# A convolution, SwiGLU and ELU kernel on one core: a lag of two units in the joined stage, DMA landings reckoned by size, and GpSimd as the maker of some convolution taps

## The chip, the cores and the metric

The kernel runs on one core of one Trainium2 chip. The metric is the device time of one launch in microseconds (us); smaller is better. An engine of the core (TensorE, VectorE, ScalarE, GpSimd; PE, DVE, ACT, POOL in the rows) works through a queue of its own in order, and an instruction that waits for a semaphore holds up all that stands behind it in that queue. SyncE (SP) issues the DMAs, also in order.

## What is computed

```python
x_unf = x_pad[:, idx, :].reshape(B, S, K, H, group)      # B=2, S=4096, D=192, K=7, H=8
out = np.einsum('hk,bskhg->bshg', softmax(weight), x_unf)  # a causal convolution of 7 taps, one set per head
x = out.reshape(B * S, D)                                  # 8192 tokens of 192 channels
x = (silu(x @ w_gate) * (x @ w_val)) @ w_out               # d_ff = 1536
h = x @ w_in                                               # d_ff = 2048
out = np.where(h > 0, h, np.exp(np.minimum(h, 0)) - 1) @ w_out2
```

The weights come as float64, the tokens as float32. Products are made to float32 precision from pieces: each operand is split in a high part (`hi`, type fp32r) and a rest (`lo`), and three of the four products are summed.

## The kernel before

**Blocks, units and pairs.** The tokens are cut into 16 blocks of 512. Channels lie on the partitions: 0:128 in a 128x512 tile, 128:192 in halves. A unit of layer 1, written (1, b, j) or s(b, j) here, is block b times 128 columns of d_ff: `swiglu(b, j)` makes two PSUM tiles, `pg` and `pv`, with nine couples of matmuls (`Into.nine`, L363), each couple two matmuls on the two 64-row halves of the array at once. A couple is called a pair below. ACT takes silu of `pg` (L679), DVE multiplies by `pv` (`gate`, L683), `split` makes hi on ACT (L653) and lo on DVE (L657), and `products_out` adds the unit's five pairs (`OutOf.ten`, L406) to the four sums `c` of the block. There are 12 units per block in layer 1, and 16 in layer 2 (`elus`, two at a time).

**Preparation.** A block's x comes by DMA (`load_x`, L519). `conv(b, 0)` makes channels 0:128: the first tap on ACT (L574), six more on DVE (L577, multiply and add in one instruction). `conv(b, 1)` makes channels 128:192 in the same way at 256 columns; for blocks 0 and 1 TensorE does that part with diagonal matrices (`products`, L553, tile `pc`). Then hi and lo are cut (L450 and L454 for 128x512, L475 and L478 for the halves), and DMAs from SBUF to SBUF copy halves across partitions (`turn`, L497; `send`, L491), so that each half of the array has its rows.

**Weights.** Each of the 34 pieces (`piece`) is brought once by DMA (L263; four moves of 64 partitions, or one of 384 KB), put together from the words of float64 by ACT (L267, L290) and DVE (L294, L275), and split into hi on ACT (L299) and lo on DVE (L302). All of it is done in the first 120 us, beside the matmuls of blocks 0 and 1.

**Order.** Nothing is scheduled by hand. `plan.add` records each operation with its engine, an estimated pitch (how long it holds its engine) and an estimated `ready` time (when its result is there); `Plan.run` walks through the estimates and emits instructions in the order that comes out, longest remaining path first among those that can start. TensorE's order alone is the order in which the units are written (`behind` links each PE task to the one before). An instruction that comes later than estimated still stands at its place in the queue.

**The joined stage.** `both_first` writes blocks 0 and 1 of layer 1 together, since the weights come too slowly for one block alone: units of block 0 alone up to j = JOINED, then one of block 1 after each one of block 0. `due` holds units whose `products_out` is not written yet:

```python
for j in range(NU[1]):
    swiglu(0, j)
    if due:
        for u in due.pop(0):
            products_out(u)
    due.append([(1, 0, j)])
    if j >= JOINED:
        swiglu(1, done)
```

So with the lag of one, TensorE's order is s(0,0), s(0,1), products of (0,0), s(0,2), products of (0,1), and so on.

Of the kernel before, what the change touches and what calls it, by code (L numbers as in the profile page):

```python
# [7 lines left out]
F32 = mybir.dt.float32  # L8
# [4 lines left out]
ALU = mybir.AluOpType  # L13
# [3 lines left out]
P = 128  # L17
# [3 lines left out]
LEAD = 3  # L21
AIDED = 1
PATIENCE = 0.05
JOINED = 4
EPS = 2.0**-16
SPARED = range(0, 34)

# [5 lines left out]
class Task:  # L33
# [3 lines left out]
    def __init__(self, engine, pitch, ready, emit):  # L37
        self.engine, self.pitch, self.ready, self.emit = engine, pitch, ready, emit
        self.drain = 0.05 if engine in ("act", "dve") else 0.0
        self.needs, self.behind, self.left, self.next, self.at, self.tail = [], [], 0, [], None, 0.0  # L40


class Plan:
# [60 lines left out]
    def run(self, free, patience):  # L104

        self.link()
        waiting = {e: [] for e in free}
        for t in self.tasks:
            if not t.left:
                waiting[t.engine].append((0.0, t))  # L110
        count = 0
        while any(waiting.values()):
            when, e = min((max(free[e], min(a for a, _ in w)), e) for e, w in waiting.items() if w)
            can = [(a, t) for a, t in waiting[e] if a <= when + patience]
            a, t = max(can, key=lambda c: c[1].tail)
            waiting[e].remove((a, t))
            t.at = max(when, a)
            free[e] = t.at + t.pitch
            t.emit()
            count += 1  # L120
            for d in t.next:
                d.left -= 1
                if not d.left:
                    at = 0.0
                    for q in d.needs:
                        at = max(at, q.at + (q.pitch + q.drain if q.engine == d.engine else q.ready))
                    for q in d.behind:
                        at = max(at, q.at)
                    waiting[d.engine].append((at, d))
        assert count == len(self.tasks)  # L130
# [3 lines left out]
def tile_conv_swiglu_elu(ctx: ExitStack, tc: tile.TileContext, x, weight, words, out, FF1, FF2):  # L134
# [42 lines left out]
    def pool(emit, needs=(), new=(), uses=(), pitch=1.45, ready=1.6):  # L177
        return plan.add("pool", pitch, ready, emit, needs, new, uses)

    def move(emit, needs=(), new=(), uses=(), pitch=0.62, ready=2.9):  # L180
        return plan.add("sp", pitch, ready, emit, needs, new, uses)

    def couple(emit, needs=(), new=(), uses=()):
        return plan.add("pe", 0.233, 0.64, emit, needs, new, uses)
# [65 lines left out]
    def piece(k, moves, halves, serves):  # L250
# [50 lines left out]
        def lo_part(pick, hi, lo):  # L301
            nc.vector.tensor_tensor(out=lo, in0=pick(box["f"]), in1=raw(hi), op=ALU.subtract)  # L302

        came = [
            move(lambda i=i: bring(i), new=[st_b] if i == 0 else (), uses=[] if i == 0 else [st_b], ready=3.3)
            for i in range(len(moves))
        ]
        for i in came[1:]:
# [111 lines left out]
    class Operand:  # L420
# [25 lines left out]
        def write(self, s, value, needs, uses, n):  # L446


            def hi():
                nc.scalar.copy(self.tile(0)[:, s, :n], value())  # L450

            def lo():
                v, h = value(), self.tiles[0][:, s, :n]
                nc.vector.tensor_tensor(out=self.tile(1)[:, s, :n], in0=v, in1=raw(h), op=ALU.subtract)  # L454

            h = self.task(0, act, hi, needs, uses)
            l = self.task(1, dve, lo, [*needs, h], [self.bufs[0], *uses])
            self.slots[0, s], self.slots[1, s] = [h], [l]
            if s == 0:
                for q, done in ((0, h), (1, l)):  # L460
                    self.slots[q, 1] = [
                        move(lambda q=q, r=r, r_in=r_in: turn(self.tiles[q], r, r_in, n), [done], uses=[self.bufs[q]])
                        for r, r_in in ((lower, upper), (upper, lower))
                    ]

        def spread(self, value, done, buf, n):


            half = n // 2
            places = (lower, slice(0, half)), (upper, slice(half, n))  # L470
            his, los = [], []
            for r, c in places:

                def hi(r=r, c=c):
                    nc.scalar.copy(self.tile(0)[r, 2, c], value()[r, :half])  # L475

                def lo(r=r, c=c):
                    nc.vector.tensor_tensor(  # L478
                        out=self.tile(1)[r, 2, c], in0=value()[r, :half], in1=raw(self.tiles[0][r, 2, c]), op=ALU.subtract
                    )  # L480

                h = self.task(0, act, hi, [done], [buf], pitch=0.33, ready=0.45)
                l = self.task(1, dve, lo, [done, h], [self.bufs[0], buf], pitch=0.34, ready=0.47)
                his.append(h)
                los.append(l)
            for q, own in enumerate((his, los)):
                other = []
                for (r, c), (r_in, _), t in zip(places, places[::-1], own):

                    def send(q=q, r=r, c=c, r_in=r_in):  # L490
                        nc.sync.dma_start(out=raw(self.tiles[q][r_in, 2, c]), in_=raw(self.tiles[q][r, 2, c]))  # L491

                    other.append(move(send, [t], uses=[self.bufs[q]]))
                self.slots[q, 2] = [*own, *other]

    def turn(t, r, r_in, n):
# [2 lines left out]
    def load_x(b):  # L499
# [12 lines left out]
        def bring(k):  # L512
# [6 lines left out]
            nc.sync.dma_start(out=at(k, skip, HALO + m), in_=src)  # L519

        came = [
            move(lambda k=k: bring(k), new=[] if k else [buf], uses=[buf] if k else [], ready=3.2) for k in range(3)
        ]
        pads = []
        if a:
# [11 lines left out]
    def products(b):  # L537
# [20 lines left out]
            t = plan.add("pe", cost, cost + 0.4, lambda k=k: product(k), [diagonals[k], *came[1]], **new)  # L558
        X[b].spread(lambda: box["p"], t, bank, n)

    def conv(b, g):

        n = blocks[b][2]
        m, c0 = ((n, 0), (n // 2, HALO + TB))[g]
        src, src_b, came = xs[b]
        acc_b = plan.buffer("cv", 2)
        box = {}

        def tap(k):
            s = src["t"][:, c0 + k : c0 + k + m]  # L570
            w = taps[:, g, k : k + 1]
            if k == HALO:
                box["acc"] = cv_p.tile([P, TB], F32, tag="cv", name=f"cv{b}_{g}")
                nc.scalar.mul(box["acc"][:, :m], s, w)  # L574
                return
            acc = box["acc"][:, :m]
            nc.vector.scalar_tensor_tensor(out=acc, in0=s, scalar=w, in1=acc, op0=ALU.mult, op1=ALU.add)  # L577

        less = 0.0 if g == 0 else 0.27
        t = act(lambda: tap(HALO), [made, *came[g]], new=[acc_b], uses=[src_b], pitch=0.62 - less, ready=0.78 - less)  # L580
        for k in range(HALO):
            t = dve(lambda k=k: tap(k), [t], uses=[src_b, acc_b], pitch=0.67 - less, ready=0.8 - less)
        if g == 0:
            if b not in X:
                X[b] = Operand(f"x{b}", home["x", b])
            X[b].write(0, lambda: box["acc"][:, :n], [t], [acc_b], n)
        else:
            X[b].spread(lambda: box["acc"], t, acc_b, n)
# [281 lines left out]
    def both_first():  # L870
# [3 lines left out]
        waiting = []  # L874
        for j in range(NU[1]):
            swiglu(0, j)
            if due:
                for u in due.pop(0):
                    products_out(u)
            due.append([(1, 0, j)])  # L880
            if j >= JOINED:
                swiglu(1, done)
                waiting.append([(1, 1, done)])
                done += 1
# [82 lines left out]
```

## Time and profile before

| | |
|---|---|
| median of 3 runs | 1224.97 us (1223.95 to 1226.94) |
| the profiled execution | 1224.98 us |
| its span, first to last instruction | 1223.2 us (so 1.8 us lie around it) |
| TensorE busy in the span | 1208.4 us (99%) |
| VectorE busy | 981.6 us (80%) |
| ScalarE busy | 833.7 us (68%) |
| GpSimd busy | 2.1 us |
| DMA from HBM, mean over the span | 21 GB/s read and written |

TensorE is busy nearly throughout, so time can be won or lost only where it waits: at the start, and at waits inside. VectorE's 80% is a mean over a start in which it is nearly full and a long rest in which it is not. The rows give the start of an instruction in us from the span's start, how long it took, the idle time of its engine just before it in brackets, and what ended that.

### The profile page before, as it was taken

The page shows a single profiled execution, that of the slowest core. Times are in us where ns is not written, and L with a number is a line of the kernel's source. Part 1 is how long each engine was busy: PE and PEld are TensorE (multiplying, and loading weights), DVE is VectorE, ACT ScalarE, POOL GpSimd, SP SyncE. Part 2 cuts the span into 40 slices and gives each one's busy share as a digit, 9 for nine tenths or more (in the row PEclk, how much of TensorE's full clock was granted, in tenths as well). Part 3 has the DMA queues.
Part 4 walks back from the last instruction along what each step waited for, and adds up shares of the span by engine and source line. Part 5 has one row for each costly group of instructions (what it writes and reads, how often), then busy time and mean ns, then how long its engine had stood idle before and what let it go on. Part 6 is the DMA issues. An engine that isn't in the chain of part 4 may idle for free.

```text
span 1223.2 us, 25355 instructions
## 1 busy us (share of the span) xinstructions
PE 1208.4 (99%) x10272; PEld 1023.3 (84%) x10272; DVE 981.6 (80%) x1631; ACT 833.7 (68%) x1556; POOL 2.1 (0%) x15
## 2 busy tenths in 40 slices
PE   7999999999999999999999999999999999999998
PEld 5878888999999999988888888878878888888876
DVE  8899899788595986959779596895968869495697
ACT  7878687486683856748576484765848667385676
POOL 0000000000000000000000000000000000000000
PEclk9999999999999999999999999999999999999999
DMA  5736020202020020201102011020200102000000
GB/s 162 200 95 162 15 44 14 66 18 53 1 44 27 18 53 8 50 15 25 47 10 49 14 36 36 18 53 1 44 14 18 40 1 48 11 18 14 18 10 18
DMA packets 34917, 48.65 MB, mean 40 GB/s; under 512 B 5872, under 2 KB 19696, under 8 KB 34800
## 3 DMA queue, kind: packets, MB, share of 16 engines
q1 hardware_dynamic: 34784, 47.04, 15.2%
q8 instruction: 80, 1.31, 0.5%
q14 instruction: 37, 0.30, 0.1%
q10 hardware_dynamic: 16, 0.00, 0.0%
HBM read 19.75 MB, written 6.29 MB: 21 GB/s over the span
## 4 chain that ended last, share of the span: by engine, by line
PE 88%; DVE 4%; ACT 3%; DMA 2%; SPq 1%; issue 1%; ACTq 0%; DVEq 0%
PE c L406 39%; PE pv L363 21%; PE ph L363 20%; PE pg L363 7%; DMA words<-in_words_dram 2%; DVE t L721 1%; SPq L263 1%; DVE t L725 1%; DVE h L657 1%; DVE cv L577 1%; ACT t L679 0%; DVE t L683 0%; ACT words L290 0%; ACT h L653 0%; SPq L519 0%
## 5 line engine op out<-in xcount | busy, mean ns | idle before, releaser
L406 PE MATMUL c<-h,out 64*128 64x512 f32 x4400 | 624.2, 392 | 2.7 <-ACT h L653 1.7
L406 PEld LDWEIGHTS c<-h,out 64*128 64x128 f32 x4400 | 482.4, 185 | 82.6 <-DVE o L762 3.7
L653 ACT CAST h<-t 128x512 fp32r<-128x512 f32 x440 | 274.2, 624 | 172.0 <-DVE t L683 124.3
L363 PE MATMUL pv<-x,in1hi 64*128 64x512 f32 x1152 | 390.6, 393 | 0.4 <-DVE t L683 0.3
L363 PE MATMUL pg<-x,in1hi 64*128 64x512 f32 x1152 | 390.0, 393 | 0.5 <-ACT in1hi L299 0.5
L657 DVE TENSOR_TENSOR h<-t,h 128x512 fp32r<-128x512 f32 x440 | 302.8, 688 | 92.4 <-ACT h L653 89.4
L363 PE MATMUL ph<-y,in2hi 64*128 64x512 f32 x1536 | 316.4, 391 | 0.0
L363 PEld LDWEIGHTS ph<-y,in2hi 64*128 64x128 f32 x1536 | 234.2, 185 | 26.9 <-DVE t L725 0.8
L363 PEld LDWEIGHTS pv<-x,in1hi 64*128 64x128 f32 x1152 | 213.2, 185 | 33.5 <-DVE t L683 1.3
L363 PE MATMUL ph<-y,in2lo 64*128 64x512 f32 x768 | 233.8, 391 | 0.0
L363 PE MATMUL pg<-x,in1lo 64*128 64x512 f32 x576 | 226.1, 393 | 0.8 <-DVE in1lo L302 0.8
L363 PE MATMUL pv<-x,in1lo 64*128 64x512 f32 x576 | 226.2, 393 | 0.0
L683 DVE TENSOR_TENSOR t<-t,pv 128x512 f32<-128x512 f32 x192 | 131.6, 685 | 117.7 <-ACT t L679 117.4
L363 PEld LDWEIGHTS pg<-x,in1hi 64*128 64x128 f32 x1152 | 213.1, 185 | 8.3 <-ACT in1hi L299 1.3
L679 ACT ACTIVATE t<-pg 128x512 f32<-128x512 f32 x192 | 114.6, 597 | 148.8 <-PE pg L363 142.2
L721 DVE SCALAR_TENSOR_TENSOR t<-t,th 128x512 f32<-128x512 f32 x256 | 175.7, 687 | 9.7 <-ACT t L717 9.2
L725 DVE SCALAR_TENSOR_TENSOR t<-ph,t 128x512 f32<-128x512 f32 x256 | 172.1, 688 | 3.0
L713 ACT ACTIVATE th<-ph 128x512 f32<-128x512 f32 x256 | 153.7, 600 | 24.5 <-PE ph L363 23.6
L717 ACT ACTIVATE t<-ph 128x512 f32<-128x512 f32 x256 | 153.9, 601 | 0.0
L363 PEld LDWEIGHTS ph<-y,in2lo 64*128 64x128 f32 x768 | 137.3, 185 | 12.4
L363 PEld LDWEIGHTS pv<-x,in1lo 64*128 64x128 f32 x576 | 106.7, 185 | 16.4
L363 PEld LDWEIGHTS pg<-x,in1lo 64*128 64x128 f32 x576 | 106.7, 185 | 5.1 <-DVE in1lo L302 1.6
(66 smaller groups left out, 566.1 us busy)
## 6 DMA issues: line engine op xcount, KB each, us to landing
x<-x SPq DMA_DIRECT2D x64, 128.0 KB, 3.4
y<-y SPq DMA_DIRECT2D x64, 128.0 KB, 2.3
words<-in_words_dram SPq DMA_DIRECT2D x14, 384.0 KB, 3.9
words<-in_words_dram SPq DMA_DIRECT2D x40, 128.0 KB, 3.0
x<-x SPq DMA_DIRECT2D x64, 64.0 KB, 2.0
out_dram<-o SPq DMA_DIRECT2D x16, 256.0 KB, 2.0
xs<-in_x_dram SPq DMA_DIRECT2D x14, 259.0 KB, 2.9
words<-in_words_dram SPq DMA_DIRECT2D x40, 64.0 KB, 2.6
```

The costliest lines, as they stand in the source:

```text
L263: nc.sync.dma_start(out=to[r, g], in_=w[r_in, g_in])
L363: nc.tensor.matmul(p[:, :n], w[r, k, s], m[r, s, :n], start=i == 0, stop=i == len(seq) - 1)
L406: nc.tensor.matmul(p[:, :n], lhs[r], m[r, :n], start=start, stop=stop)
L577: nc.vector.scalar_tensor_tensor(out=acc, in0=s, scalar=w, in1=acc, op0=ALU.mult, op1=ALU.add)
L653: nc.scalar.copy(parts[u][0][:, :n], live[u][0]["t"][:, :n])
L657: nc.vector.tensor_tensor(out=parts[u][1][:, :n], in0=live[u][0]["t"][:, :n], in1=raw(parts[u][0][:, :n]), op=ALU.subtract)
L679: nc.scalar.activation(out=box["t"][:, :n], in_=box["p"][0][:, :n], func=AF.Silu)
L683: nc.vector.tensor_tensor(out=t, in0=t, in1=box["p"][1][:, :n], op=ALU.mult)
L713: nc.scalar.activation(out=own["th"][:, :n], in_=box["p"][a][:, :n], func=AF.Tanh, scale=0.5)
L717: nc.scalar.activation(out=own["t"][:, :n], in_=box["p"][a][:, :n], func=AF.Exp)
L721: nc.vector.scalar_tensor_tensor(out=t, in0=t, scalar=1.0, in1=th, op0=ALU.add, op1=ALU.mult)
L725: nc.vector.scalar_tensor_tensor(out=t, in0=box["p"][a][:, :n], scalar=0.0, in1=t, op0=ALU.max, op1=ALU.min)
```

## The change

Four things are edited; all else is as before.

1. **The lag** in `both_first`: `if due:` becomes `if len(due) > 1:`, so a unit's products are written two units after it. JOINED goes from 4 to 5: one unit more of block 0 stands alone ahead of the first unit of block 1.
2. **Landings by size**: `move` takes `kb`, and `Plan.run` reckons a DMA's landing from a running total (`flow`) instead of a fixed time after its issue. These are estimates: they change the order that is emitted, not a transfer.
3. **`calm`**: in blocks 1 and 2 (`CALM`), `conv(b, 0)`, and in block 2 `conv(b, 1)` too, are made by GpSimd: one multiplication for the first tap, then six times a multiplication into a tile `by` and an addition to the sum. ACT's L574 and the six L577 of DVE fall away for each of these three (two of 128x512, one of 128x256). The later steps (hi on ACT, lo on DVE, the copies) stay.
4. The pitches of some moves are given apart (0.45 or 0.60 for 0.62).

```diff
--- before.py
+++ after.py
@@ -21,7 +21,9 @@
 LEAD = 3
 AIDED = 1
 PATIENCE = 0.05
-JOINED = 4
+CALM = (1, 2)
+FLOW = 250
+JOINED = 5
 EPS = 2.0**-16
 SPARED = range(0, 34)
 
@@ -37,6 +39,7 @@
     def __init__(self, engine, pitch, ready, emit):
         self.engine, self.pitch, self.ready, self.emit = engine, pitch, ready, emit
         self.drain = 0.05 if engine in ("act", "dve") else 0.0
+        self.kb = 0
         self.needs, self.behind, self.left, self.next, self.at, self.tail = [], [], 0, [], None, 0.0
 
 
@@ -108,7 +111,7 @@
         for t in self.tasks:
             if not t.left:
                 waiting[t.engine].append((0.0, t))
-        count = 0
+        count, flow = 0, 0.0
         while any(waiting.values()):
             when, e = min((max(free[e], min(a for a, _ in w)), e) for e, w in waiting.items() if w)
             can = [(a, t) for a, t in waiting[e] if a <= when + patience]
@@ -116,6 +119,9 @@
             waiting[e].remove((a, t))
             t.at = max(when, a)
             free[e] = t.at + t.pitch
+            if t.kb:
+                flow = max(t.at + t.pitch + 0.9, flow) + t.kb / FLOW
+                t.ready = flow + 0.4 - t.at
             t.emit()
             count += 1
             for d in t.next:
@@ -177,8 +183,10 @@
     def pool(emit, needs=(), new=(), uses=(), pitch=1.45, ready=1.6):
         return plan.add("pool", pitch, ready, emit, needs, new, uses)
 
-    def move(emit, needs=(), new=(), uses=(), pitch=0.62, ready=2.9):
-        return plan.add("sp", pitch, ready, emit, needs, new, uses)
+    def move(emit, needs=(), new=(), uses=(), pitch=0.62, ready=2.9, kb=0):
+        t = plan.add("sp", pitch, ready, emit, needs, new, uses)
+        t.kb = kb
+        return t
 
     def couple(emit, needs=(), new=(), uses=()):
         return plan.add("pe", 0.233, 0.64, emit, needs, new, uses)
@@ -302,7 +310,10 @@
             nc.vector.tensor_tensor(out=lo, in0=pick(box["f"]), in1=raw(hi), op=ALU.subtract)
 
         came = [
-            move(lambda i=i: bring(i), new=[st_b] if i == 0 else (), uses=[] if i == 0 else [st_b], ready=3.3)
+            move(
+                lambda i=i: bring(i), new=[st_b] if i == 0 else (), uses=[] if i == 0 else [st_b], ready=3.3,
+                kb=(160, 80, 160, 80)[i] if len(moves) > 1 else 384, pitch=0.62 if len(moves) > 1 else 0.45,
+            )
             for i in range(len(moves))
         ]
         for i in came[1:]:
@@ -459,7 +470,8 @@
             if s == 0:
                 for q, done in ((0, h), (1, l)):
                     self.slots[q, 1] = [
-                        move(lambda q=q, r=r, r_in=r_in: turn(self.tiles[q], r, r_in, n), [done], uses=[self.bufs[q]])
+                        move(lambda q=q, r=r, r_in=r_in: turn(self.tiles[q], r, r_in, n), [done], uses=[self.bufs[q]],
+                             kb=150)
                         for r, r_in in ((lower, upper), (upper, lower))
                     ]
 
@@ -490,7 +502,7 @@
                     def send(q=q, r=r, c=c, r_in=r_in):
                         nc.sync.dma_start(out=raw(self.tiles[q][r_in, 2, c]), in_=raw(self.tiles[q][r, 2, c]))
 
-                    other.append(move(send, [t], uses=[self.bufs[q]]))
+                    other.append(move(send, [t], uses=[self.bufs[q]], kb=75))
                 self.slots[q, 2] = [*own, *other]
 
     def turn(t, r, r_in, n):
@@ -519,7 +531,8 @@
             nc.sync.dma_start(out=at(k, skip, HALO + m), in_=src)
 
         came = [
-            move(lambda k=k: bring(k), new=[] if k else [buf], uses=[buf] if k else [], ready=3.2) for k in range(3)
+            move(lambda k=k: bring(k), new=[] if k else [buf], uses=[buf] if k else [], ready=3.2,
+                 kb=65 if k else 259, pitch=0.6 if k else 0.45) for k in range(3)
         ]
         pads = []
         if a:
@@ -558,6 +571,36 @@
             t = plan.add("pe", cost, cost + 0.4, lambda k=k: product(k), [diagonals[k], *came[1]], **new)
         X[b].spread(lambda: box["p"], t, bank, n)
 
+    def calm(box, src, src_b, acc_b, came, g, m, c0, b):
+
+
+
+        of = lambda k: (src["t"][:, c0 + k : c0 + k + m], taps[:, g, k : k + 1])
+        by_b = plan.buffer("th", 2)
+
+        def begin():
+            box["acc"] = cv_p.tile([P, TB], F32, tag="cv", name=f"cv{b}_{g}")
+            s, w = of(HALO)
+            nc.gpsimd.tensor_scalar_mul(out=box["acc"][:, :m], in0=s, scalar1=w)
+
+        def scaled(k):
+            if k == 0:
+                box["by"] = th_p.tile([P, TB], F32, tag="th", name=f"by{b}_{g}")
+            s, w = of(k)
+            nc.gpsimd.tensor_scalar_mul(out=box["by"][:, :m], in0=s, scalar1=w)
+
+        def added():
+            acc = box["acc"][:, :m]
+            nc.gpsimd.tensor_tensor(out=acc, in0=acc, in1=box["by"][:, :m], op=ALU.add)
+
+        one, two = 0.1 + 0.0014 * m, 0.1 + 0.0024 * m
+        t = pool(begin, [made, *came[g]], new=[acc_b], uses=[src_b], pitch=one, ready=one + 0.15)
+        for k in range(HALO):
+            place = dict(uses=[src_b, by_b]) if k else dict(uses=[src_b], new=[by_b])
+            t = pool(lambda k=k: scaled(k), [t], pitch=one, ready=one + 0.15, **place)
+            t = pool(added, [t], uses=[acc_b, by_b], pitch=two, ready=two + 0.15)
+        return t
+
     def conv(b, g):
 
         n = blocks[b][2]
@@ -577,9 +620,14 @@
             nc.vector.scalar_tensor_tensor(out=acc, in0=s, scalar=w, in1=acc, op0=ALU.mult, op1=ALU.add)
 
         less = 0.0 if g == 0 else 0.27
-        t = act(lambda: tap(HALO), [made, *came[g]], new=[acc_b], uses=[src_b], pitch=0.62 - less, ready=0.78 - less)
-        for k in range(HALO):
-            t = dve(lambda k=k: tap(k), [t], uses=[src_b, acc_b], pitch=0.67 - less, ready=0.8 - less)
+        if b in CALM:
+            t = calm(box, src, src_b, acc_b, came, g, m, c0, b)
+        else:
+            t = act(
+                lambda: tap(HALO), [made, *came[g]], new=[acc_b], uses=[src_b], pitch=0.62 - less, ready=0.78 - less
+            )
+            for k in range(HALO):
+                t = dve(lambda k=k: tap(k), [t], uses=[src_b, acc_b], pitch=0.67 - less, ready=0.8 - less)
         if g == 0:
             if b not in X:
                 X[b] = Operand(f"x{b}", home["x", b])
@@ -874,7 +922,7 @@
         waiting = []
         for j in range(NU[1]):
             swiglu(0, j)
-            if due:
+            if len(due) > 1:
                 for u in due.pop(0):
                     products_out(u)
             due.append([(1, 0, j)])
```

What this does to the order, read from the built programs of the two kernels. **On PE**, just behind unit s(0,1). The names are those of the program: `pg0_1` is the gate tile of block 0, unit 1; `x00` and `x01` are the hi and lo parts of block 0's x; `c1_0_k` are the sums of layer 1, block 0. Before:

```order
L363 MATMUL pg0_1_269<-x01_200,in1hi_114 128x512
L363 MATMUL pv0_1_270<-x01_200,in1hi_114 128x512
L406 MATMUL c1_0_0_308<-h0_1_0_0_298,out1_118 128x512
L406 MATMUL c1_0_1_309<-h0_1_0_0_298,out1_118 128x512
L406 MATMUL c1_0_0_308<-h1_1_0_0_306,out1_118 128x512
```

and now:

```order
L374 MATMUL pg0_1_282<-x01_206,in1hi_114 128x512
L374 MATMUL pv0_1_283<-x01_206,in1hi_114 128x512
L374 MATMUL pg0_2_315<-x00_198,in1hi_114 128x512
L374 MATMUL pv0_2_316<-x00_198,in1hi_114 128x512
L374 MATMUL pg0_2_315<-x00_198,in1lo_115 128x512
```

The nine pairs of s(0,2) stand ahead of the products of (0,0), which follow behind them.

**On ACT**, around the hi of block 0's x (`words0`, `w0` and so on are pieces of weights; `pc0` is the TensorE-made part of x). Before:

```order
L267 ACTIVATE w0_189<-words0_136 128x384
L450 CAST x00_193<-cv0_0_153 128x512
L290 ACTIVATE words0_136<-words0_136 128x384
L475 CAST x00_193<-pc0_157 64x256 x2
L290 ACTIVATE words1_173<-words1_173 128x384
L267 ACTIVATE w1_216<-words1_173 128x384
L299 CAST in1hi_114<-w0_189 128x384
```

and now:

```order
L275 ACTIVATE w0_187<-words0_134 128x384
L298 ACTIVATE words0_134<-words0_134 128x384
L461 CAST x00_198<-cv0_0_154 128x512
L298 ACTIVATE words1_169<-words1_169 128x384
L307 CAST in1hi_114<-w0_187 128x384
L487 CAST x00_198<-pc0_156 64x256 x2
```

The hi of the first piece of weights stands ahead of the `pc0` part of x now, and so does an instruction that waits for `words1` to land.

**On ACT**, where the hi of block 2's x stands (`cv2_0` and `cv2_1` are the sums that GpSimd makes now; `t1_0_11` and `h0_1_0_11` belong to the last unit of block 0). Before:

```order
L679 ACTIVATE t1_0_11_1071<-pg0_11_1040 128x512
L450 CAST x20_1080<-cv2_0_735 128x512
L653 CAST h0_1_0_11_1097<-t1_0_11_1071 128x512
L679 ACTIVATE t1_1_7_1118<-pg1_7_1082 128x512
L475 CAST x20_1080<-cv2_1_862 64x256 x2
```

and now:

```order
L727 ACTIVATE t1_0_11_1078<-pg0_11_1035 128x512
L461 CAST x20_1086<-cv2_0_740 128x512
L487 CAST x20_1086<-cv2_1_867 64x256
L701 CAST h0_1_0_11_1109<-t1_0_11_1078 128x512
L487 CAST x20_1086<-cv2_1_867 64x256
L617 ACTIVATE cv3_0_1123<-xs3_766,taps_106 128x512
L727 ACTIVATE t1_1_6_1135<-pg1_6_1089 128x512
```

The silu of unit s(1,6) and the hi of (0,11) stand behind two instructions that wait for GpSimd's sums.

## Rows read from the trace of the kernel before

**Rows 1.** The page's first part: busy us, share of the span, instructions.
```profile
PE 1208.4 (99%) x10272; PEld 1023.3 (84%) x10272; DVE 981.6 (80%) x1631; ACT 833.7 (68%) x1556; POOL 2.1 (0%) x15
```
**Rows 2.** Windows: us, busy by engine, granted clock (PEclk), DMA share, GB/s.
```profile
15.00:37.00 22.00, 18.68 (x130) 13.54 (x132) 19.86 (x38) 14.90 (x32) 0.00 (x0) 0.92 0.63 167
60.00:75.00 15.00, 14.67 (x123) 11.28 (x121) 14.90 (x28) 11.49 (x25) 0.00 (x0) 1.00 0.24 75
75.00:120.00 45.00, 44.37 (x380) 35.63 (x378) 43.93 (x88) 38.20 (x82) 0.00 (x0) 1.00 0.59 155
```
**Rows 3.** The timeline of PE, 5 to 30 us: start, us, instruction, idle before.
```profile
5.77 9.10 PE L553 MATMUL pc<-xs,tapped 128*128 128x256 f32 x28 [0.91 <-ACT tapped L544]
...
15.42 0.50 PE L363 MATMUL pg<-x,in1hi 64*128 64x512 f32 x1 [0.54 <-ACT in1hi L299]
...
18.89 0.47 PE L363 MATMUL pg<-x,in1hi 64*128 64x512 f32 x1
...
20.99 0.39 PE L363 MATMUL pv<-x,in1hi 64*128 64x512 f32 x1
23.12 0.50 PE L406 MATMUL c<-h,out 64*128 64x512 f32 x2 [1.74 <-ACT h L653]
23.85 1.20 PE L406 MATMUL c<-h,out 64*128 64x512 f32 x8 [0.23 <-DVE h L657]
...
29.09 1.32 PE L406 MATMUL c<-h,out 64*128 64x512 f32 x10
```
**Rows 4.** The timeline of ACT: the first tap of block 1.
```profile
8.45 0.72 ACT L574 ACTIVATE cv<-xs,taps 128x512 f32<-128x512 f32 x1
```
**Rows 5.** The timelines of ACT and DVE, 12 to 23 us.
```profile
12.21 0.74 ACT L475 CAST x<-pc 64x256 fp32r<-64x256 f32 x2
14.85 0.51 ACT L299 CAST in1hi<-w 128x384 fp32r<-128x384 f32 x1 [0.88 <-DVE w L275]
...
18.59 3.11 DVE L577 SCALAR_TENSOR_TENSOR cv<-xs,taps,cv 128x512 f32<-128x512 f32 x4
21.73 0.69 DVE L683 TENSOR_TENSOR t<-t,pv 128x512 f32<-128x512 f32 x1
22.45 0.62 ACT L653 CAST h<-t 128x512 fp32r<-128x512 f32 x1 [2.01 <-DVE t L683]
```
**Rows 6.** DMA issues on SP's timeline, a load on PE, median landing of xs.
```profile
13.27 2.46 SPq L491 DMA_DIRECT2D x<-x  x4
15.79 1.23 SPq L497 DMA_DIRECT2D x<-x  x2
18.79 0.18 PEld L363 LDWEIGHTS pv<-x,in1hi 64*128 64x128 f32 x1 [0.42 <-DMA x<-x]
...
45.79 1.54 SPq L519 DMA_DIRECT2D xs<-in_x_dram  x3
...
xs<-in_x_dram SPq DMA_DIRECT2D x14, 259.0 KB, 2.9
```
**Rows 7.** Groups on POOL: line, shapes, count, busy us, mean ns of one.
```profile
L198 POOL MEMSET scratch<- 8x256 f32 x1 | 0.3, 302 | 0.0
L208 POOL TENSOR_SCALAR_AFFINE_SELECT scratch<-scratch 128x128 f32<-128x128 f32 x1 | 0.3, 295 | 0.1
L207 POOL MEMSET scratch<- 128x128 f32 x1 | 0.2, 195 | 0.0
```
**Rows 8.** The timeline of PE: the first of 18 pairs in a row, and the last.
```profile
37.14 0.39 PE L363 MATMUL pg<-x,in1hi 64*128 64x512 f32 x1
...
41.10 0.39 PE L363 MATMUL pg<-x,in1hi 64*128 64x512 f32 x1
```
**Rows 9.** Groups of DVE's taps over the span: count, busy us, mean ns.
```profile
L577 DVE SCALAR_TENSOR_TENSOR cv<-xs,taps,cv 128x512 f32<-128x512 f32 x96 | 71.7, 747 | 0.8
L577 DVE SCALAR_TENSOR_TENSOR cv<-xs,taps,cv 128x256 f32<-128x256 f32 x84 | 40.3, 479 | 0.6
```
**Rows 10.** The timeline of ACT at 59 us.
```profile
58.87 0.55 ACT L290 ACTIVATE words<-words 128x384 uint32<-128x384 uint32 x1 [2.03 <-DMA words<-in_words_dram]
```

## The prediction, made before the changed kernel ran

> **What bounds the kernel now.** I began with the first part of the page [rows 1]: TensorE is busy 1208.4 of 1223.2 us. Of its 10272 matmuls 28 make the `pc` part of x and 4 the taps; the other 10240 are 5120 pairs. Eighteen pairs that nothing holds up take 3.96 us from the first to the last start [rows 8], so a pair costs 3.96 / 17 = 0.233 us and all of them 1193 us. That part isn't touched. What the change can move is the rest: the start up to 15.4 us, and the waits of TensorE.
>
> The windows and the timeline of PE show where these are. In the stretch from 15 to 37 us PE is busy 18.7 of 22 us and its granted clock is 0.92 in the mean [rows 2]; there are only two levels, full and half, so some 22 x 0.08 x 2 = 3.5 us of it ran at half the clock, 1.2 GHz. Three things cost time there [rows 3]. The nine pairs of s(0,0) need 3.5 us instead of 2.1 (15.42 to 18.89), since they wait for the lo of the first weights and for copied halves of x. Behind s(0,1), whose last pair starts at 20.99, the products of (0,0) come only at 23.12 and their second pair at 23.85: 1.9 + 0.5 us lost. From there the 14 pairs up to 29.09 take 6.0 us instead of 3.3: the lo of further weights, and the half clock. After that PE is nearly full: from 60 to 120 us it idles 0.33 + 0.63 = 1.0 us [rows 2]. So 6.5 us are lost in front and 1 us behind; this is the ceiling, whatever the change intends.
>
> Why the products come late is in the timelines of ACT and DVE [rows 5]: the hi of (0,0) starts at 22.45 after 2.01 us of idling for the gate, and the gate starts at 21.73, right behind four taps of block 1 that hold DVE from 18.59 for 3.11 us. DVE's queue is the bound of this stretch, busy 19.9 of 22 us and 14.9 of 15 from 60 to 75 us [rows 2].
>
> **The change, part by part.**
>
> *Unit s(0,0).* The `pc` matmuls hold PE until about 14.7 (5.77 + 9.10, less the pipelined end of the last) [rows 3], so the first pair can come 0.7 us earlier than 15.42, when ACT has the first hi before that. It gains nothing: the last pairs of the unit wait for the copied halves of x, a weight load at 18.79 for such a DMA [rows 6]. The copies start from the `pc` part of x, which ACT casts at 12.21 [rows 5]. In the new order one cast of 0.51 us and an instruction that waits for `words1` stand ahead of it. The cost is 0.4 us (the cast, less what overlaps) if these words are there at 11.7, and 1.0 if they come at 12.3; I take 0.9, since four moves from SP take 2.5 us [rows 6] and these are behind all of the first piece. The sends and turns behind it (13.27 to 17.0 on SP) shift with it. Pair 9, the first of s(0,1), goes from 18.89 to 19.8.
>
> *The lag.* Behind s(0,1) the nine pairs of s(0,2) stand in place of the products of (0,0). s(0,1) and s(0,2) end at 19.8 + 18 x 0.233 = 24.0. The products then need silu, gate, hi and lo of (0,0): four instructions of 0.6 to 0.7 us from about 20.6, done by 23.3. So the 2.4 us go, and pair 32 comes at 19.8 + 23 x 0.233 = 25.2 instead of 29.09 [rows 3]. What is late next is the lo of the weights of s(0,3) and s(0,4): on DVE seven instructions of at most 0.69 us stand between the gate of (0,0), at about 21.3, and the first of these, so it ends near 26.0 instead of 25.4 where it is wanted. I take 0.7 us there and 0.9 at the next one, with 0 and 3 us as the bounds of both. Pair 74, which before came nine pairs after 37.14 [rows 8], at 39.2, then comes at 25.2 + 42 x 0.233 + 1.6 = 36.6: 2.6 us won. Of what was lost before, the 3.5 us at half the clock cost some 1.4 (half of it, less the waits that fall into it). They came after a stretch with waits of 1 to 2 us; between pairs 0 and 9 there are such waits again. I take one such stretch in the new kernel too: 2.6 - 1.4 = 1.2 us remain (bounds: 0 and 2.6).
>
> JOINED = 5 only moves the first unit of block 1 behind s(0,5); its pairs are the same.
>
> *Taps off DVE.* DVE no longer makes twelve taps of 0.747 and six of 0.479 us [rows 9], 11.8 us together, 4.5 of them ahead of pair 74; ACT loses three instructions. That gain is already in the walk above, where no tap stands between the casts and the gate. In block 2 it meets a PE with 1.0 us of idling left.
>
> *Taps on GpSimd.* The trace has no such instruction on POOL. Its nearest rows [rows 7]: a fill of 128 columns takes 0.195 and one of 256 columns 0.302 us, so 0.84 ns a column; a select that reads 128 columns 0.295. For a multiplication of 512 columns the ends are 0.52 (the fill with that slope) and 1.18 (four selects); I take 0.62, the select with that slope, because the two fills show that most of a short one is a fixed part. For the addition with two inputs: 0.52 and 2.36 (twice the upper end), and 1.05 taken (the slope twice). Block 1 is then 7 x 0.62 + 6 x 1.05 = 10.6 us; its x is there at 8.45 at the latest, where ACT reads it [rows 4]; so done near 19 (15 to 31). On ACT its hi stands behind the silu of (0,2), at 24.4 in the walk: no wait. Block 2 has 6.5 us more for the halves (0.40 and 0.62 each): 17.1 us (11 to 34). Its x is issued at 45.79 before [rows 6]; four moves of weights more stand ahead, 2.5 us; with a landing after 2.9 us it starts at 51.2 and ends at E = 68.3. On ACT its hi stands right behind the silu of (0,11), which comes near 69: no wait either. This is the tightest place. Behind it in ACT's queue are the hi of (0,11) and the silu of s(1,6), whose bank s(1,8) needs at pair 240, 36.6 + 166 x 0.233 = 75.3; from E to that bank it is six instructions, 3.1 us. So E up to 72.2 is free, and each us after costs one.
>
> *Landings.* The estimates cost nothing themselves. ACT waits 2.03 us for words at 58.87 [rows 10], one of the things behind the idle 1.0 us; whether a new order cures it, the order can't tell. I take 0, bounds -1.0 and +1.0.
>
> **The sum.** The profiled execution took 1224.98 us, 1223.2 of span and 1.8 around it, the same as the median of 1224.97. 1224.98 - 1.2 = 1223.8.
>
> **The rivals.**
> - *GpSimd shuts DVE out* (slower). The two would be busy together for 10.6 + 17.1 = 27.7 us. Nearly all that DVE does there reads two tiles of SBUF (the words, the lo parts); only gates and the `pc` rests read one operand from PSUM. If a GpSimd instruction holds up such a DVE instruction for its whole length, DVE loses 27.7, gets back 11.8 for the taps, finds some 3 us of its own idling [rows 2], and a third of the rest goes on beside: 27.7 - 11.8 - 3 = 12.9, of which 8.6 remain. PE follows DVE nearly one to one there. Time: 1223.8 + 8.6 = 1232.4. It decides from about 5 us on. For it: DVE has no slack at 60 to 75 us. Against it: no row shows the two hindering each other. The Trainium skill says it outright (SBUF — State Buffer, "Who interferes with whom"): a DVE instruction with two SBUF inputs contends with a GpSimd instruction that reads SBUF, and the second to start waits out the first. By that rule this rival is the outcome; no run here shows it as yet, since GpSimd was idle.
> - *ACT waits for GpSimd at (0,11)* (slower): with the middles of my ends, 0.85 and 1.7 us, block 2 takes 24.2 us, E = 75.4, and PE loses 3.2: 1227.0, and 10 us more at the upper ends.
> - *Faster*: no half clock (-1.4), the idle 1.0 behind goes, and half of the 1.6 in front: 1220.6.
>
> **Chances.** Forecast (1223.8, own range 1221.3 to 1227): 0.44. Shut out: 0.30. ACT's wait: 0.10. Faster: 0.16. By 0.3%, 3.7 us, which is about what a measurement of this kernel can tell from no change: faster 0.16, the same 0.46 (the forecast, and a little of the second rival), slower 0.38. The range reaches from the faster case to the shut-out: 1220.5 to 1234.
>
> **What would show it.** Right: PE without a long wait between s(0,1) and s(0,2); pair 32 near 25; GpSimd's instructions at 0.6 and 1.1 us, and DVE's beside them as long as before. Wrong: DVE's L302 and L705 at more than 0.8 us, or gaps between them while GpSimd runs; ACT idle ahead of L461 for GpSimd at 70 us; PE waits at 60 to 80 us.

## The result, and the profile after

The changed kernel takes 1241.57 us (median; 1240.74 to 1242.95), the kernel before beside it 1225.88. The ratio is 1.0132, 95% interval 1.0119 to 1.0145: slower by 1.3%, outside the range of 1220.5 to 1234. The profiled execution took 1241.61 us, 1239.9 of it span, 16.7 more than before.

Lines moved with the edit. L363 is now L374, L406 L417, L299 and L302 L307 and L310, L294 L302, L275 L283, L450 and L454 L461 and L465, L475 L487, L653 and L657 L701 and L705, L679 and L683 L727 and L731. GpSimd's first tap is L584, its multiplications L590, its additions L594.

The page's first part, as [rows 1]:

```profile
PE 1214.2 (98%) x10272; PEld 998.4 (81%) x10272; DVE 985.0 (79%) x1613; ACT 832.7 (67%) x1553; POOL 59.8 (5%) x54
```

DVE has 18 instructions fewer and yet is busy 3.4 us longer (981.6 before). What was left became slower. The windows, as [rows 2], with columns PE, PEld, DVE, ACT, POOL, clock, DMA share, GB/s:

```profile
15.00:37.00 22.00, 18.69 (x112) 12.77 (x114) 21.01 (x32) 14.85 (x33) 15.10 (x9) 0.77 0.55 148
60.00:75.00 15.00, 12.24 (x98) 8.53 (x94) 14.97 (x24) 10.10 (x22) 14.55 (x10) 1.00 0.39 108
75.00:120.00 45.00, 36.77 (x284) 29.40 (x284) 35.50 (x66) 29.23 (x63) 16.27 (x15) 0.89 0.45 123
```

From 60 to 75 us DVE is as full as before but finishes 24 instructions for 28, and PE falls from 14.67 to 12.24 us. From 75 to 120 us DVE and ACT themselves idle: something else is waited for there.

Where the time went is read from the starts of the same pair (counted in PE's order) in PE's timelines, in us. The forecasts are those of the prediction's walk. The last two columns are two experiments below: the change without GpSimd's part, and the change with GpSimd planned at its measured pace. Each column is one profiled execution.

| pair | before | forecast | after | no GpSimd | true pace |
|---|---|---|---|---|---|
| 9 | 18.89 | 19.8 | 22.10 | 19.58 | 21.82 |
| 32 | 29.09 | 25.2 | 30.19 | 26.63 | 30.27 |
| 74 | 39.23 | 36.6 | 41.33 | 38.69 | 41.07 |
| 150 | 56.89 | | 59.80 | 56.95 | 59.58 |
| 230 | 76.42 | | 84.28 | 75.55 | 83.76 |
| 240 | 78.74 | 75.3 | 95.23 | 77.87 | 86.10 |
| 400 | 117.18 | | 134.16 | 117.15 | 126.41 |
| 5119 | 1217.64 | | 1234.28 | 1217.64 | 1226.67 |

After against before: +2.1 us up to pair 74, +0.8 to 150, +5.0 to 230, +8.6 between 230 and 240, and +0.2 over all the rest. GpSimd works from 7.7 to 30.8 and from 55.3 to 91.6 us: the first and the third step lie there, the second mostly in between, and the fourth is one wait and a stretch at the half clock behind it. PE's timeline of after, for [rows 3]:

```profile
16.86 0.79 PE L374 MATMUL pg<-x,in1lo 64*128 64x512 f32 x1 [1.44 <-DVE in1lo L310]
...
23.57 0.79 PE L374 MATMUL pg<-x,in1lo 64*128 64x512 f32 x1 [0.35 <-DVE in1lo L310]
...
84.28 1.55 PE L417 MATMUL c<-h,out 64*128 64x512 f32 x10
92.63 2.80 PE L417 MATMUL c<-h,out 64*128 64x512 f32 x10 [6.80 <-ACT h L701]
```

PE has no long wait between s(0,1) and s(0,2), as forecast, but it waits for lo parts of weights from DVE, and for 6.80 us for the hi of (0,11). Behind that wait ten matmuls take 2.80 us instead of 1.55. The granted clock of 0.89 from 75 to 120 us puts 45 x 0.11 x 2 = 9.9 us at the half level; the wait itself takes up a part of these. PE's waits for these lo parts and for the gate, added up over the span (us in all, times, longest):

```profile
PE pv L374 <- DVE t L731: 4.2, 6, 0.9
PE pg L374 <- DVE in1lo L310: 2.5, 3, 1.4
```

The first is PE waiting for the gate to free the PSUM tile `pv`. Before, these two came to 0.3 and 0.8 us.

GpSimd's groups, for [rows 7]:

```profile
L590 POOL TENSOR_SCALAR by<-xs,taps 128x512 f32<-128x512 f32 x12 | 23.0, 1920 | 0.7
L594 POOL TENSOR_TENSOR cv<-cv,by 128x512 f32<-128x512 f32 x12 | 16.9, 1409 | 0.8
L590 POOL TENSOR_SCALAR by<-xs,taps 128x256 f32<-128x256 f32 x6 | 7.4, 1241 | 0.1
L594 POOL TENSOR_TENSOR cv<-cv,by 128x256 f32<-128x256 f32 x6 | 5.3, 886 | 0.3
```

The multiplication of 512 columns took 1.92 us where 0.62 was taken (1.18 the upper end), the addition 1.41 (1.05; 2.36). The same groups while DVE stood idle, 82.4 to 90.3 us:

```profile
L590 POOL TENSOR_SCALAR by<-xs,taps 128x256 f32<-128x256 f32 x3 | 2.8, 918 | 0.0
L594 POOL TENSOR_TENSOR cv<-cv,by 128x512 f32<-128x512 f32 x2 | 2.5, 1266 | 0.0
L590 POOL TENSOR_SCALAR by<-xs,taps 128x512 f32<-128x512 f32 x1 | 1.6, 1557 | 0.0
L594 POOL TENSOR_TENSOR cv<-cv,by 128x256 f32<-128x256 f32 x2 | 1.5, 727 | 0.2
```

So undisturbed it is 1.56 and 1.27 us, by one and two instructions. The rest comes while DVE is busy; ACT was idle in that stretch, too, and no run sets DVE's share apart. And GpSimd holds up DVE in turn. First four additions on POOL's timeline, then the four DVE instructions that start beside them:

```profile
11.43 1.50 POOL L594 TENSOR_TENSOR cv<-cv,by 128x512 f32<-128x512 f32 x1
...
14.86 1.52 POOL L594 TENSOR_TENSOR cv<-cv,by 128x512 f32<-128x512 f32 x1
...
18.32 1.58 POOL L594 TENSOR_TENSOR cv<-cv,by 128x512 f32<-128x512 f32 x1
...
65.92 1.40 POOL L594 TENSOR_TENSOR cv<-cv,by 128x512 f32<-128x512 f32 x1
```

```profile
11.71 1.64 DVE L302 SCALAR_TENSOR_TENSOR w<-w,words 128x384 int32<-128x384 int32 x1
...
15.18 1.62 DVE L310 TENSOR_TENSOR in1lo<-w,in1hi 128x384 fp32r<-128x384 f32 x1
...
18.69 1.63 DVE L302 SCALAR_TENSOR_TENSOR w<-w,words 128x384 int32<-128x384 int32 x1
...
66.20 1.53 DVE L283 SCALAR_TENSOR_TENSOR w<-words,w 128x384 int32<-128x384 int32 x1
```

Before, the same three kinds of instruction take 0.55 us in the mean (L294, L275 and L302 there):

```profile
L294 DVE SCALAR_TENSOR_TENSOR w<-w,words 128x384 int32<-128x384 int32 x33 | 18.1, 555 | 1.9 <-ACT w L267 1.3 <-ACT words L290 0.5
L275 DVE SCALAR_TENSOR_TENSOR w<-words,w 128x384 int32<-128x384 int32 x31 | 17.0, 554 | 0.2
...
L302 DVE TENSOR_TENSOR in1lo<-w,in1hi 128x384 fp32r<-128x384 f32 x12 | 6.6, 553 | 0.0
```

The additions end at 12.93, 16.38, 19.90 and 67.32, the DVE instructions at 13.35, 16.80, 20.32 and 67.73: each time 0.41 to 0.42 us later. In these four cases the DVE instruction does its work when the addition is over. *load_add* below has many more: of its 28 DVE instructions of 384 columns that start during an addition, 27 end 0.41 to 0.42 us behind it.

Last, GpSimd's last addition for block 2 on POOL's timeline, and ACT's timeline at the wait:

```profile
90.65 0.97 POOL L594 TENSOR_TENSOR cv<-cv,by 128x256 f32<-128x256 f32 x1
```

```profile
80.25 0.58 ACT L727 ACTIVATE t<-pg 128x512 f32<-128x512 f32 x1
89.70 0.62 ACT L461 CAST x<-cv 128x512 fp32r<-128x512 f32 x1 [8.87 <-POOL cv L594]
91.65 0.40 ACT L487 CAST x<-cv 64x256 fp32r<-64x256 f32 x1 [1.34 <-POOL cv L594]
91.96 0.61 ACT L701 CAST h<-t 128x512 fp32r<-128x512 f32 x1
```

That addition ends at 90.65 + 0.97 = 91.62. Until then ACT's queue stands, with the hi of (0,11) (91.96), which PE wants, behind it.

### The profile page after: what moved, and what is told of

The parts are those of the page before. It is cut to its first block, busy times and chain, and to the rows that moved or that the text cites. A ratio compares the mean times of both kernels' runs of the same rounds, so it can differ in the third digit from the quotient of the medians.

```text
span 1239.9 us, 25369 instructions
## 1 busy us (share of the span) xinstructions
PE 1214.2 (98%) x10272; PEld 998.4 (81%) x10272; DVE 985.0 (79%) x1613; ACT 832.7 (67%) x1553; POOL 59.8 (5%) x54
## 4 chain that ended last, share of the span: by engine, by line
PE 88%; DVE 4%; POOL 3%; issue 1%; ACT 1%; SPq 1%; DMA 1%; DVEq 0%; ACTq 0%; POOLq 0%
PE c L417 40%; PE pv L374 27%; PE ph L374 20%; PE pg L374 2%; POOL by L590 2%; POOL cv L594 1%; DVE t L769 1%; SPq L271 1%; DVE t L773 1%; DMA words<-in_words_dram 1%; DVE h L705 0%; DVE w L302 0%; DMA xs<-in_x_dram 0%; POOL cv L584 0%; ACT th L761 0%
## 5 line engine op out<-in xcount | busy, mean ns | idle before, releaser
L417 PE MATMUL c<-h,out 64*128 64x512 f32 x4410 | 631.4, 393 | 7.2 <-ACT h L701 6.8
L417 PEld LDWEIGHTS c<-h,out 64*128 64x128 f32 x4410 | 477.5, 185 | 97.7 <-ACT h L701 7.2
L374 PE MATMUL pv<-x,in1hi 64*128 64x512 f32 x1152 | 394.4, 396 | 4.2 <-DVE t L731 4.2
L374 PE MATMUL pg<-x,in1hi 64*128 64x512 f32 x1152 | 392.6, 395 | 1.6 <-ACT in1hi L307 0.9
L701 ACT CAST h<-t 128x512 fp32r<-128x512 f32 x441 | 274.4, 623 | 172.3 <-DVE t L731 124.6
L705 DVE TENSOR_TENSOR h<-t,h 128x512 fp32r<-128x512 f32 x441 | 303.3, 688 | 94.9 <-ACT h L701 92.0
L374 PE MATMUL ph<-y,in2hi 64*128 64x512 f32 x1536 | 319.2, 391 | 0.0
L374 PEld LDWEIGHTS ph<-y,in2hi 64*128 64x128 f32 x1536 | 237.5, 185 | 31.2 <-DVE t L773 0.3
L374 PEld LDWEIGHTS pv<-x,in1hi 64*128 64x128 f32 x1152 | 214.8, 186 | 51.4 <-DVE t L731 7.8
L374 PE MATMUL ph<-y,in2lo 64*128 64x512 f32 x768 | 241.8, 391 | 0.0
L374 PE MATMUL pg<-x,in1lo 64*128 64x512 f32 x576 | 228.8, 397 | 2.6 <-DVE in1lo L310 2.5
L374 PE MATMUL pv<-x,in1lo 64*128 64x512 f32 x576 | 227.7, 395 | 0.0
L731 DVE TENSOR_TENSOR t<-t,pv 128x512 f32<-128x512 f32 x192 | 131.1, 683 | 120.8 <-ACT t L727 120.5
L374 PEld LDWEIGHTS pg<-x,in1hi 64*128 64x128 f32 x1152 | 214.7, 186 | 5.9 <-DVE w L283 1.4
L727 ACT ACTIVATE t<-pg 128x512 f32<-128x512 f32 x192 | 114.4, 596 | 149.2 <-PE pg L374 143.5
L374 PEld LDWEIGHTS ph<-y,in2lo 64*128 64x128 f32 x768 | 141.2, 185 | 14.3
L374 PEld LDWEIGHTS pv<-x,in1lo 64*128 64x128 f32 x576 | 107.6, 187 | 21.8
L374 PEld LDWEIGHTS pg<-x,in1lo 64*128 64x128 f32 x576 | 107.6, 187 | 5.7 <-DVE in1lo L310 4.8
```

The lines of the kernel that those rows point to most:

```text
L374: nc.tensor.matmul(p[:, :n], w[r, k, s], m[r, s, :n], start=i == 0, stop=i == len(seq) - 1)
L417: nc.tensor.matmul(p[:, :n], lhs[r], m[r, :n], start=start, stop=stop)
L701: nc.scalar.copy(parts[u][0][:, :n], live[u][0]["t"][:, :n])
L705: nc.vector.tensor_tensor(out=parts[u][1][:, :n], in0=live[u][0]["t"][:, :n], in1=raw(parts[u][0][:, :n]), op=ALU.subtract)
L727: nc.scalar.activation(out=box["t"][:, :n], in_=box["p"][0][:, :n], func=AF.Silu)
L731: nc.vector.tensor_tensor(out=t, in0=t, in1=box["p"][1][:, :n], op=ALU.mult)
```

## The experiments

**The change without GpSimd's part, and with one block of it.** Theory: everything lost comes from GpSimd, by holding DVE up and by the wait at (0,11). Rival: the lag or the landings lose, too.

```diff
-CALM = (1, 2)
+CALM = ()        # no_calm;  (1,) in calm_1;  (2,) in calm_2
```

*no_calm*: 

> The change without GpSimd's part (CALM empty): lag, JOINED = 5 and the reckoned landings alone. Theory (all of the loss comes from GpSimd: its late sums and its hold on DVE): within 2 us of the kernel before, 1223.5 to 1226, and pair 74 at 38 to 39.5. Rival (the new order in front costs the 2.1 us seen at pair 74): 1227 to 1228.5.

*calm_1*: 

> GpSimd makes block 1 alone. Theory: the loss of the front stays (some 2 us at pair 74) and that of 60 to 95 us goes: 1226.5 to 1229. Rival (the two blocks share the loss evenly): 1232 to 1234.

*calm_2*: 

> GpSimd makes block 2 alone. Theory: the wait at (0,11) of 7 us and the 5 to 6 us between pairs 130 and 230 stay, the front is that of the kernel without GpSimd's part: 1236 to 1240. Rival (the wait at (0,11) came from the late start of the stretch before it): below 1232.

Measured: 1225.0 us without GpSimd (ratio 0.9995, 0.9986 to 1.0004), 1228.97 with block 1 alone (1.003, 1.0019 to 1.0041), 1239.49 with block 2 alone (1.0114, 1.01 to 1.0128). All of the loss comes with GpSimd's part, and the two blocks nearly add up: 1225.0 + 4.0 + 14.5 = 1243.5, against 1241.57. In block 2's run ACT waits at the same cast, though another order starts GpSimd at 34.10 us in place of 55.29:

```profile
70.00 0.62 ACT L461 CAST x<-cv 128x512 fp32r<-128x512 f32 x1 [5.52 <-POOL cv L594]
```

**The change with GpSimd planned at its measured pace.** The planner puts ACT's cast where it reckons that the sum is there; only these numbers change.

```diff
-        one, two = 0.1 + 0.0014 * m, 0.1 + 0.0024 * m
+        one, two = 0.1 + 0.0034 * m, 0.3 + 0.0022 * m
```

*true_pace*: 

> The changed kernel, but the planner is told GpSimd's pace as measured under load (a multiplication of 512 columns 1.84 us, an addition 1.43), so that the casts of block 2 stand later in ACT's queue. Theory (two causes: ACT's wait at (0,11), about 7 to 8 us, and DVE held up by GpSimd, about 8): the wait goes and the hold stays, 1232 to 1235. Rival (the waits for GpSimd's sums are all of it, the hold is hidden): 1224 to 1227.

Measured: 1233.68 us, ratio 1.007 (1.0055 to 1.0085). The wait is gone, and with it 7.9 us; ACT goes straight on to the hi that PE wants:

```profile
79.74 0.58 ACT L727 ACTIVATE t<-pg 128x512 f32<-128x512 f32 x1
81.78 0.62 ACT L701 CAST h<-t 128x512 fp32r<-128x512 f32 x1 [1.46 <-DVE t L731]
```

8.2 us above the 1225.46 beside it remain, and GpSimd's chains are as long as ever (23.7 and 37.9 us). So the loss is ACT's wait, 7.9 us, and another 8.2 us, which the next runs trace to DVE's hold.

**Idle work on GpSimd, in the kernel before.** Is it GpSimd's presence that costs, or how the order changed around it? Here the order of ACT, DVE, PE and the DMA issues is that of before, and `ballast` gives GpSimd a chain of instructions on a tile that nobody reads any more. DVE keeps its taps. The second part was planned for the landing of block 2's x; but it reads nothing of x, and in the traces GpSimd runs on without a pause, from 13 or 14 us to 66 (fills), 72 (both), 76 (additions) and 78 us (multiplications). So it also works in the 24 us in which it is idle in the change.

```diff
+        if g == 0 and b in (1, 2):
+            ballast([*came[0], multiplied[1]], {1: [...], 2: [...]}[b])
```

with, for blocks 1 and 2, multiplications and additions mixed; 40 and 60 fills; 14 and 21 multiplications; 17 and 26 additions.

*load_both*: 

> The kernel before, all taps where they were, plus idle work on GpSimd that nobody waits for: 7 + 6 multiplications and additions of 448 columns on a constant tile, and 13 + 12 more at 448 and 224 columns behind the landing of block 2's x, much as in the change. Theory (GpSimd's instructions hold up DVE's with two inputs in SBUF, and DVE has no slack): 1232 to 1240, more than the hold of the change itself, since DVE keeps its taps here; L302 and L705 stretched beside an addition. Rival (it was only the wait of ACT for the sums, and the late order): 1224 to 1227.

*load_fill*: 

> The same, but the idle work is 40 + 60 fills of 448 columns, which write SBUF and read nothing, for about as long. Theory (the hold comes from GpSimd reading SBUF): 1224 to 1227, and L302 and L705 as long as before. Rival (any traffic of GpSimd holds DVE up): as slow as with multiplications and additions, 1230 or more.

*load_mul*: 

> The same, but only multiplications with one tensor input (14 + 21 of 448 columns). Theory (a multiplication holds a DVE instruction up by 0.3 to 0.4 us, an addition for its whole length): 1226 to 1231, clearly less than with additions. Rival (each GpSimd instruction holds alike): the same as with additions.

*load_add*: 

> The same, but only additions with two tensor inputs (17 + 26 of 448 columns). Theory: 1233 to 1245, the dearest of the four; L302 and L705 at 1.2 to 1.7 us beside one. Rival (each GpSimd instruction holds alike): the same as with multiplications alone.

Measured beside 1224.99 us, with 981.6 us of DVE busy in the kernel before:

| | GpSimd busy with it, us | DVE busy, us | time, us | ratio (95%) |
|---|---|---|---|---|
| load_fill | 47.4 | 981.1 | 1225.45 | 0.9999 (0.9987 to 1.001) |
| load_mul | 61.4 | 987.1 | 1228.52 | 1.0026 (1.0017 to 1.0036) |
| load_both | 35.1 + 20.6 | 995.3 | 1234.83 | 1.0073 (1.0058 to 1.0088) |
| load_add | 59.1 | 1014.0 | 1254.41 | 1.0233 (1.0217 to 1.0248) |

The theory holds; only the additions cost more than its 1245. The time follows DVE: with additions DVE is busy 32.4 us longer, and the kernel takes 29.4 us more. DVE's groups in the three pure cases, over 15 to 75 us for fills and additions and 15 to 80 for multiplications (line, shapes, count, busy us, mean ns; in these kernels L302 is the lo of the weights, as before, and L702 the gate). With fills:

```profile
L702 DVE TENSOR_TENSOR t<-t,pv 128x512 f32<-128x512 f32 x17 | 11.6, 681 | 0.6 <-ACT t L698 0.6
...
L302 DVE TENSOR_TENSOR in1lo<-w,in1hi 128x384 fp32r<-128x384 f32 x12 | 6.6, 552 | 0.0
```

With multiplications:

```profile
L702 DVE TENSOR_TENSOR t<-t,pv 128x512 f32<-128x512 f32 x18 | 12.2, 676 | 0.0
...
L302 DVE TENSOR_TENSOR in1lo<-w,in1hi 128x384 fp32r<-128x384 f32 x12 | 8.0, 669 | 0.0
```

With additions:

```profile
L302 DVE TENSOR_TENSOR in1lo<-w,in1hi 128x384 fp32r<-128x384 f32 x8 | 10.3, 1292 | 0.0
L702 DVE TENSOR_TENSOR t<-t,pv 128x512 f32<-128x512 f32 x7 | 4.7, 676 | 0.0
```

L302 reads two tiles of SBUF: 0.55, 0.67 and 1.29 us. The gate reads one of its operands from PSUM: 0.68 in all three. Fills write SBUF and hold nobody up. This agrees with the rule of the Trainium skill ("SBUF — State Buffer", "Who interferes with whom") that a DVE instruction with two SBUF inputs contends with a GpSimd instruction that reads SBUF, not with one that only writes it. In one point the measurement differs from the rule as the prediction put it: the multiplication reads SBUF as well, and holds L302 up by 0.12 us in the mean and 0.36 at most, not until its end.

**What DVE's relief is worth.** If GpSimd had disturbed nobody, what would the change have brought? Here the 18 taps are made by nobody.

```diff
-            for k in range(HALO):
+            for k in range(0 if b in (1, 2) else HALO):
```

*fewer_new* (in no_calm): 

> The lag, JOINED = 5 and the landings without GpSimd, and DVE's 18 taps of blocks 1 and 2 (the ones that the change took from DVE) are left out: only the first tap is made, by ACT. So this is what the change would be if GpSimd made its taps at once and disturbed nobody. Theory (DVE's queue is the bound of the joint stage up to 120 us, busy 99 of 105 us from 15 to 120, and swallows what the lag wins in front): 11.8 us less work on it give 3 to 6 us, 1219 to 1222. Rival (DVE is busy but PE's remaining waits are those of single chains and landings): 1223 to 1226.

*fewer_old* (in the kernel before): 

> The kernel before, with the same 18 taps of DVE left out. Theory: here the wait between s(0,1) and s(0,2) stays or shrinks with the taps that stood before the gate, so 1220 to 1223, a gain within 2 us of the one with the lag. Rival (the lag is what counts, once DVE has room): 1224 to 1226, while the kernel with the lag is at 1219 to 1222.

Measured beside 1225.68: 1224.0 us with the lag (0.9983, 0.9974 to 0.9992) and 1223.36 without (0.9974, 0.9964 to 0.9985). The theory, which called DVE's queue the bound up to 120 us, fell: 11.8 us taken from it bring 1.0 beside the 1225.0 of no_calm, and 2.3 in the kernel before. The rival's range holds with the lag; without it the time lies between the two ranges. Windows of no_calm and then of fewer_new:

```profile
15.00:120.00 105.00, 100.56 (x819) 84.12 (x821) 99.25 (x194) 84.39 (x183) 0.00 (x0) 0.98 0.58 156
```

```profile
15.00:120.00 105.00, 102.25 (x823) 79.63 (x825) 96.69 (x191) 86.18 (x188) 0.00 (x0) 0.98 0.58 156
```

DVE is nearly as busy with fewer instructions to do, since later work moves up: its 95% was not all needed by PE at that time. What PE waits for in no_calm is mostly single chains, above all the copies of x in s(0,0):

```profile
16.01 0.47 PE L374 MATMUL pg<-x,in1hi 64*128 64x512 f32 x1 [1.30 <-DMA x<-x]
17.28 0.47 PE L374 MATMUL pg<-x,in1hi 64*128 64x512 f32 x1 [0.42 <-DMA x<-x]
...
27.53 0.50 PE L374 MATMUL pg<-x,in1lo 64*128 64x512 f32 x1 [0.40 <-DVE in1lo L310]
```

**The lag alone, and the landings alone.**

```diff
-CALM = (1, 2)
+CALM = ()         # both
-JOINED = 5
+JOINED = 4        # both
-            if t.kb:
+            if False:          # onlylag
-            if len(due) > 1:
+            if due:            # onlyflow
```

*onlylag*: 

> The kernel before with the lag of two units alone (JOINED = 4, landings at fixed times, pitches as changed, taps on DVE). Theory (what the lag wins in front is given back where DVE is the bound): pair 32 some 2 us earlier than before, 1224 to 1227. Rival (the lag wins and the landings lose): 1221 to 1223.

*onlyflow*: 

> The kernel before with the landings by size and the pitches alone (JOINED = 4, lag of one, taps on DVE). Theory: 1224 to 1227, with the wait of PE behind s(0,1) still there. Rival (the landings' order loses what the lag wins): 1227 to 1230.

Both runs keep the pitches of the moves as changed. Measured beside 1225.68: 1224.51 us (0.9991, 0.9982 to 0.9999) and 1225.29 (0.9993, 0.9985 to 1.0002): the same as before within 0.3%, as the theory has it. With the lag alone pair 32 starts at 26.22, 2.9 us earlier than before, and pair 400 at 117.04, 0.1 us earlier. Where no_calm gives its lead back is seen in the table: 2.5 us at pair 32, 0.5 at 74, 0.9 at 240, none at 400. Of these two and no_calm the lag alone has the lowest time, but their intervals overlap, and its 0.1% against the kernel before is at the edge of what was measured.

## Why the prediction was wrong

*What bounds the kernel, the ceiling.* The 1.2 us that the forecast took of the ceiling are of the right size: without GpSimd the kernel is at 1225.0, and with the taps for nothing at 1224.0, against a forecast of 1223.8. The ceiling of 7.5 us itself is a little high: the half microsecond before 23.85 stands in the 6.0 us up to 29.09 once more, and by pairs the front loses 29.09 - 15.42 - 32 x 0.233 = 6.2 us, not 6.5. No run here comes near it. "PE follows DVE nearly one to one" was right for a loss (29.4 us for 32.4 in *load_add*) and wrong for a gain (1.0 us for 11.8).

*s(0,0) and the lag.* Without GpSimd pair 9 came at 19.58 (19.8 forecast), pair 32 at 26.63 (25.2), pair 74 at 38.69 (36.6, from which the sum then took 1.4 off for a half-clock stretch): the wait for the products went, and of the 3.9 us forecast at pair 32 2.5 were there, of the 2.6 at pair 74 0.5; waits for copies and weights and a half-clock stretch (0.92 in the window, as in [rows 2]) took the rest. That nothing is given back after pair 74 was a silent step that failed, too: by pair 400 no lead is left. In the changed kernel block 1's additions delayed the lo of the first weights (L310 at 15.18, 1.62 us), and the clock of 15 to 37 us fell to 0.77.

*GpSimd's costs: mis-sized.* 0.62 was taken for the multiplication, and its upper end was 1.18; it took 1.56 undisturbed and 1.92 in the mean. The choice rested on fills and selects [rows 7], none of which reads a tile with a number per partition. The addition's 1.05 became 1.27 and 1.41. Block 1's chain took 23.2 us (10.6 forecast), block 2's 36.3 (17.1; 34 the upper end). Block 2's began at 55.29 (51.2). Four more moves of weights stood ahead of its x, as counted (49 in SP's order, 45 before); but SP's queue itself waited for ACT and DVE, 4.7 us from 25 to 52 us in place of 1.3 from 25 to 47 before, and the landing took 3.7 us in place of 2.9:

```profile
40.27 11.22 SPq L271 DMA_DIRECT2D words<-in_words_dram  x16
51.60 0.52 SPq L531 DMA_DIRECT2D xs<-in_x_dram  x1
```

So E was 91.6 instead of 68.3, and what the prediction had named as the tightest place gave way. E up to 72.2 was free, which leaves 19.4 us late; PE itself came to pair 230 at 84.28, 11.4 us later than the walk has it (36.6 + 156 x 0.233 = 72.9), and the 8.0 between them are the size of the wait's 7.9.

*Two rivals in place of one.* Two steps of the forecast failed: it put the hold of DVE by GpSimd at nothing, and by too low a cost of GpSimd's instructions it had block 2's sums ready before ACT wanted them. The runs showed 8.2 us for the hold (what remains in true_pace) and 7.9 for ACT's wait. Both slower rivals came true at once, by the rows named for them: L302 and L310 at up to 1.65 us and L705 at up to 1.25, PE short of work from 60 to 75 us, and ACT idle ahead of L461 (from 80.8 to 89.7 us, where 70 was named). "Shut out" was priced at 8.6 us; 8.2 remain with the true pace. That the size fits is partly luck: it let GpSimd hold DVE up for all of 27.7 us, where the 22.2 us of additions do most of it, and they were longer than forecast. "ACT waits" was priced at 3.2 from the middles of ends that were too low; it cost 7.9. The range failed because the two were weighed as alternatives, 0.30 and 0.10. They share a cause in part: beside a busy DVE GpSimd's instructions are longer, so a hold makes the sums late too. But the price alone was enough: by the undisturbed times above block 2 takes 7 x 1.56 + 6 x 1.27 + 7 x 0.92 + 6 x 0.73 = 29.3 us (an estimate), and E is 84.6, still past 72.2. Together the rivals would have stood at 1223.8 + 8.6 + 3.2 = 1235.6, and the range ended at 1234.

*Landings.* 0 was taken; the landings with the pitches measure 0 (0.9993, an interval with 1 in it).

## What to carry to other kernels

Before work is moved from DVE to GpSimd, look at what DVE does beside it: if its instructions read two SBUF tiles and PE waits for them, an addition on GpSimd is paid for on DVE with more than half of its length (32.4 us for 59.1 in *load_add*), whoever waits for the sum. Price an instruction that no row shows by a run of it alone, since one in-order queue behind a late result (ACT's, here) turns the error into a stall. And take the busy share of an engine for a bound only if taking work away from it moves the end.

## What the runs showed of the hardware

- On GpSimd the multiplication by a number per partition is slower than the addition of two tiles: 1.56 against 1.27 us at 128x512, 0.92 against 0.73 at 128x256, with DVE idle (one to three instructions each).
- The hold of a DVE instruction with two SBUF inputs by a GpSimd addition ends with the addition, and 0.41 to 0.42 us of its own work follow at 384 columns: four cases in the change and 27 of 28 in *load_add*. The gate, with one operand in PSUM, takes 0.68 us beside additions as without them.
- GpSimd is slower beside a busy DVE: 1.99 us for the multiplication between 55 and 82 us, against 1.56 with DVE (and ACT) idle:

```profile
L590 POOL TENSOR_SCALAR by<-xs,taps 128x512 f32<-128x512 f32 x5 | 9.9, 1987 | 0.2
```
